# Opening of an FFT-mixing and maxout kernel: half the filter doubling by DMA, the second half of the weights loaded later, zT in parts

## The chip, the cores and the metric

One core of a Trainium2 chip runs the whole program. Its engines work side by side, each on its own queue of instructions in order, and wait for each other by semaphores: TensorE (PE, matmuls; PEld is its weight load), VectorE (DVE), ScalarE (ACT), GpSimd (POOL) and SyncE (SP, which only issues DMAs here; GpSimd issues DMAs too). The metric is the device time of one execution in microseconds (us), less is better.

## The reference

The input x has 8 batches of 3072 positions by 256 channels. Each batch goes through a real FFT along the positions, is multiplied by a filter (`filt_r + i filt_i`, one value per frequency and channel), and is transformed back. Each of the 24576 resulting tokens then goes through a small expert layer with 1024 hidden units.

```
X = np.fft.rfft(x, axis=1)
Y = X * (filt_r + 1j * filt_i)
y = np.fft.irfft(Y, n=3072, axis=1)          # tokens of 256 channels
h1, h2 = y @ w1, y @ w2                      # 256 x 1024 each
out = np.maximum(h1, h2) @ w_out             # 1024 x 256
```

## The kernel before, in words

**The transform as matmuls.** The FFT of 3072 = 96 x 32 is made of small matmuls with tables of sines: C1 (96 points) and U (32 points with the twiddles) forward, VP, VQ (32) and G1 (96) backward. All tables are made at the start of the kernel from index ramps (`table_c`, `tables_u`, `sines_u`, `table_v`, `table_g`). The filter multiplies the half-transformed data elementwise: `product` forms `pq = px * F`, with px in PSUM (the output of `s2`) and F, the filter, in SBUF. F is loaded into partitions 0 to 31 of each half (`load_f`, 16 DMAs that GpSimd issues) and has to stand a second time in partitions 32 to 63 (`double_f`, L124 to L131): for the frequencies w = 0 to 8 by four copies on VectorE (L128), for w = 8 to 12 by four DMAs on SyncE (L130). `fix_f` (L145) sets one row by hand.

**The expert layer.** max(h1, h2) = relu(h1 - h2) + h2. So the kernel keeps Wd = w1 - w2 (`prep_wd`, four parts on GpSimd, L298), computes ph = y Wd (L482), takes its relu into `gt` (L484 on VectorE, L486 on ScalarE) and adds gt w_out (L536) and y M, where M = w2 w_out is made once (`prep_t`, `prep_m`, from `w2b`, the cast of w2, L291).

**Batch 0 by a short way.** Batches 1 to 7 pass through DRAM between the stages of the transform while the expert layer of the batch ahead runs. Batch 0 has nothing to hide behind: it is done at once in SBUF, and this is the opening. Its steps are `s1t` (first matmuls, as the x loads land), `t1` (transposes into `bt`), six times `s2` (matmuls with U into px), `product` (two for each v from 0 to 5, s = 0 and s = 1), `s3t` (matmuls with VP and VQ; evicted to zT, L595 and L597), then `t2` (transposes of zT into `zr`, four rows at a time), and `s4` (matmuls with G1 into py; evicted as `y_`, L464 on ScalarE and L466 on VectorE). The first `ph` needs both halves of the first y tile.

**Who does which product.** VectorE reads px from PSUM. For the products that GpSimd does, ScalarE first copies px to SBUF (`stage_x`, tiles xs). Of the six s = 1 products GpSimd does those in POOLED = (0, 2, 3, 4) and a quarter of that of v = 5 (`shared_product`), VectorE the rest and all of s = 0.

**Order.** The order of instructions on each engine is that of the program text; nothing is rescheduled. A tile comes from a pool with a fixed number of buffers, and its first writer waits until the last reader of what lay there before is done. The pool `init` holds what only the opening needs; `setup.close()` frees it, and the pools of the main loop (`apool`, `ypool` and others) are laid over it. The weights w1 and w2 are loaded by SyncE in two halves of 512 columns (`load_w`, L287 and L288) into WS, a buffer of the long-lived pool `zrpool`.

**Behind the opening** comes the main loop over 65 tiles of 384 tokens, eight steps j each; `plan` and `mid` give the step at which each piece of other work (the remaining `t2`, `f1` of batch 1, and so on) stands. `f1(1, c)` is the first transform step of batch 1: a matmul into pa (L330), an eviction to `at` (L333, L335) and, for odd c, a DMA to DRAM (L338, SyncE). Four of them stand in front of the loop, with two `spin` matmuls that compute nothing.

On GpSimd, behind the last product, stand: the x load (1, 2), the Wo load, Wd part 0, two x loads, Wd parts 1 to 3, the two casts to `w2b`, and the table CT. On SyncE: the filter's last rows, the four doublings, the four weight loads, then the `ad` writes.

Of the kernel before, what the change touches and what calls it, by code (L numbers as in the profile page):

```python
# [8 lines left out]
FP32 = mybir.dt.float32  # L9
BF16 = mybir.dt.bfloat16  # L10
AF = mybir.ActivationFunctionType
OP = mybir.AluOpType
# [15 lines left out]
def kernel(  # L28
# [92 lines left out]
                    o_ = F[64 * g + r0:64 * g + r0 + 16, ri, w0:w1].rearrange("p w s d -> p (w s) d")  # L121
                    G.dma_start(out=o_[:, n0:n], in_=src)

    def double_f(h, g, ri, engine):  # L124
        w0, w1 = WP[h]
        o_, i_ = F[64 * g + 32:64 * g + 64, ri, w0:w1], F[64 * g:64 * g + 32, ri, w0:w1]
        if engine is V:
            V.tensor_copy(o_, i_)  # L128
        else:
            nc.sync.dma_start(out=o_, in_=i_)  # L130
# [11 lines left out]
        G.tensor_copy(F[0:32, ri, 0, 0], FZ[0:32, ri])  # L142

    def fix_f():
        V.tensor_copy(F[32:33, 0, 0, 0], FZ[32:33, 0])  # L145


    V.memset(W1, 1.0)
# [5 lines left out]
    jb = init.tile([128, 16], FP32)  # L154
    cid = init.tile([128, 128], FP32)

    hv = init.tile([128, 2, 1], FP32)
    load_x(0, 0, 1)
    G.iota(pid, pattern=[[1, 1]], base=0, channel_multiplier=1, allow_small_or_imprecise_dtypes=True)
# [32 lines left out]

    def table_ct():
        G.memset(CT, 0.0)
# [55 lines left out]

    def table_g():
        pg = ps.tile([96, NP], FP32, tag="ps", name="pg")
        TE.matmul(pg, C1, I128[0:NP, 0:NP], start=True, stop=True)
        S.activation(G1, pg, AF.Copy)

    def table_v(h, q):
# [22 lines left out]
            S.activation(tab[:, 6 * h + i0:6 * h + 6, s], pv[s][:, i0:6], AF.Copy)  # L279


    WS = zrpool.tile([128, 4, HID], FP32, tag="zr", name="WS")
    w1f, w2f = WS[:, 0:2], WS[:, 2:4]

    def load_w(h):
        js = slice(512 * h, 512 * h + 512)
        nc.sync.dma_start(out=w1f[:, :, js], in_=moe_w1.rearrange("(c p) j -> p c j", p=128)[:, :, js])  # L287
        nc.sync.dma_start(out=w2f[:, :, js], in_=moe_w2.rearrange("(c p) j -> p c j", p=128)[:, :, js])  # L288

    def cast_w2(h):  # L290
        G.tensor_copy(w2b[:, :, 512 * h:512 * h + 512], w2f[:, :, 512 * h:512 * h + 512])  # L291

    def load_wo():
        G.dma_start(out=Wo, in_=moe_w_out.rearrange("(c p) j -> p c j", p=128))

    def prep_wd(q, engine):
        js = slice(256 * q, 256 * q + 256)
        engine.tensor_tensor(Wd[:, :, js], w1f[:, :, js], w2f[:, :, js], OP.subtract)  # L298

    def prep_t(jp):  # L300
        pt = ps.tile([128, 4, D], BF16, tag="ps", name="pt")
# [18 lines left out]
    zd = {}  # L320
    at_ = {}

    def f1(b, c, engine):
        if c == 0:
# [3 lines left out]
        at = at_[b]  # L328
        pa = ps.tile([96, 2, D], FP32, tag="ps", name="pa")
        TE.matmul(pa, C1, xb[b, c // 2][:, 2 * (c % 2):2 * (c % 2) + 2], start=True, stop=True)  # L330
# [57 lines left out]
    def product(E, v, s, px, pool=None):  # L388
        pq = (pool or pqpool).tile([128, 2, 2, D], BF16, tag="pq", name="pq")
        E.tensor_tensor(pq, px.rearrange("p (o i) d -> p o i d", o=1).to_broadcast([128, 2, 2, D]),  # L390
                        F[:, :, 2 * v:2 * v + 2, s], OP.mult)
        return pq

    def shared_product(v, s, px, xs_, pool):
        pq = pool.tile([128, 2, 2, D], BF16, tag="pq", name="pq")
        V.tensor_tensor(pq[:, 0], px, F[:, 0, 2 * v:2 * v + 2, s], OP.mult)
        V.tensor_tensor(pq[:, 1, 0], px[:, 0], F[:, 1, 2 * v, s], OP.mult)
        G.tensor_tensor(pq[:, 1, 1], xs_[:, 1], F[:, 1, 2 * v + 1, s], OP.mult)
        return pq

    def s3(b, v, pq):
# [174 lines left out]

    def s3t(v, pq):
        pool, tag = (ps, "ps") if v % 2 else (pso, "po")
        pz = [pool.tile([128, 2, 2, 2, 2, NM], FP32, tag=tag, name="pt%d" % g) for g in range(2)]
        for _ in range(2 if v == 1 else 1):  # L580
            TE.matmul(pz[0].rearrange("p i s r c m -> p (i s r c m)"), W1[:, 0:128], W1, start=True, stop=True)  # L581
        for i in range(2):
            for s in range(2):
                for dc in range(2):
                    for q, tab in enumerate((VP, VQ)):
                        for g in range(2):
                            TE.matmul(pz[g][:, i, s, :, dc], pq[s][64 * g:64 * g + 64, q, i, 128 * dc:128 * dc + 128],  # L587
                                      tab[64 * g:64 * g + 64, 2 * v + i, s].rearrange("p (r m) -> p r m", r=2),
                                      start=(q == 0), stop=(q == 1))
        zv = zT.rearrange("p c m (w g) q -> p w g (c m) q", g=2)  # L590
        for g in range(2):
            o_ = zv[:, 2 * v:2 * v + 2, g]
            i_ = pz[g].rearrange("p i s r c m -> p i (c m) (s r)")
            if v >= 4 and g == 1:
                V.tensor_copy(o_, i_)  # L595
            else:
                S.activation(o_, i_, AF.Copy)  # L597

    def t2(c, engines):
        if c == 0:  # L600
# [2 lines left out]
        for k, engine in enumerate(engines):  # L603
            pr = ps.tile([96, n, D], BF16, tag="ps", name="pr")
            m0 = 4 * c + n * k
            for m in range(n):
                for dc in range(2):
                    TE.transpose(pr[:, m, 128 * dc:128 * dc + 128], zT[:, dc, m0 + m].rearrange("p u q -> p (u q)"),  # L608
                                 I128)
            if engine is V:  # L610
                V.tensor_copy(zr[0][:, m0:m0 + n], pr)
# [13 lines left out]
    for g in range(2):  # L625
        for ri in range(2):
            double_f(1, g, ri, nc.sync)
    for h in range(2):
        load_w(h)
    spin(12)  # L630
    for c in range(8):
        s1t(c)
# [4 lines left out]
        if c < 7:  # L637
            spin(2)
    bt[0] = bpool.tile([128, NU, D], BF16, tag="bt", name="bt")
    zT = bpool.tile([128, 2, NM, NU, 4], BF16, tag="bt", name="zT")  # L640
    for n in range(6):
        t1(n, S if n % 2 else V)
    put_v(0, 0, table_v(0, 0))
    for g in range(2):
        for ri in range(2):
            double_f(0, g, ri, V)
    fix_f()
    xs = {}

    def stage_x(v):  # L650
        t_ = init.tile([128, 2, D], FP32, name="xs%d" % v)
        S.activation(t_, pxs[v][1], AF.Copy)
        xs[v] = t_

    POOLED = (0, 2, 3, 4)

    def products(v):
        pool = pq0 if v > 2 else pqpool
        pq = [product(V, v, 0, pxs[v][0], pool)]
        if v == 5:  # L660
            pq.append(shared_product(v, 1, pxs[v][1], xs[v], pool))
        else:
            pq.append(product(G, v, 1, xs[v], pool) if v in POOLED else product(V, v, 1, pxs[v][1], pool))
        return pq

    pqs = {}
    pxs = {v: s2(0, v) for v in (1, 0)}
    stage_x(0)
    put_v(0, 1, table_v(0, 1))
    pxs[2] = s2(0, 2)  # L670
    stage_x(2)
    sines_u(1)
    put_v(1, 0, table_v(1, 0))
    pxs[3] = s2(0, 3)
    stage_x(3)
    put_v(1, 1, table_v(1, 1))
    for v in (1, 0, 2):
        pqs[v] = products(v)
        if v == 0:
            load_x(1, 0, 2)  # L680
# [39 lines left out]

    todo = {}
# [30 lines left out]
    plan(0, 9, prep_m)  # L752
    for c, n in ((2, 7), (4, 22), (5, 32), (6, 40), (7, 48)):
        plan(0, n, t2, c, (V,))
    plan_f1(0, 1, (5, 6, 7, 7, 9, 9, 10, 10, 11, 11, 12, 12), 13)
    plan_f2(0, (25, 28, 31, 35, 38, 42, 46), ((0,), (), (1,), (2,), (3,), (4,), (5, 6)),
            (8, 8, 10, 12, 17, 20, 24, 28), (10, 13, 16, 20, 24, 27, 30, 33))
# [71 lines left out]
```

## Time and profile before

| | |
|---|---|
| time, median of 3 runs | 497.97 us (497.71 to 498.13) |
| time of the profiled execution | 498.64 us |
| its span | 496.8 us |
| TensorE busy | 483.8 us (97%) |
| VectorE, ScalarE, GpSimd busy | 335.4, 320.4, 258.7 us |
| granted TensorE clock, mean | 0.989 |
| chain that ended last, share of TensorE | 92% |

The span is what the profile covers; the execution's own time is 1.8 us longer, and the median of the runs is 0.67 us below the profiled execution. The page's slices are a fortieth of the span each, 12.4 us, with busy shares in tenths; PEclk is the clock that was granted to TensorE. A row of a timeline has the start, the busy time, the engine, the line and the operation with its output and inputs, the shape, how many instructions are merged in the row, and in brackets the idle time ahead of the first of them with what ended it.

### The profile page before, as it was taken

Reading aid. Unit: us, or ns where it says so; the run is one execution under the profiler, and the core shown is the slowest. Engines: PE = TensorE matmul, PEld = TensorE weight load, DVE = VectorE, ACT = ScalarE, POOL = GpSimd, SP = SyncE. Lnnn points to the kernel's source line nnn. Section 1 sums busy time; section 2 is a strip of 40 time slices with the busy share of each in tenths; the row PEclk is TensorE's granted clock in tenths of the full one; section 3 lists DMA queues with packets and bytes.
Section 4 is the critical chain, followed back from the end, with each engine's and each line's share of the span. In section 5 each row is a group of like instructions: output and inputs, shape, how many; then the busy total and the mean of one; then the engine's idle time right before and its main releaser. Section 6 shows DMA issues by size and latency. Waiting matters only on the chain.

```text
span 496.8 us, 14137 instructions
## 1 busy us (share of the span) xinstructions
PE 483.8 (97%) x5759; PEld 353.5 (71%) x5759; DVE 335.4 (68%) x535; ACT 320.4 (64%) x667; POOL 258.7 (52%) x342
## 2 busy tenths in 40 slices
PE   7699999999999999999999999999999999999997
PEld 3457777777777777777777777776777777777775
DVE  7886788468855688467855688457873688556542
ACT  5777478667775677576866668665766656464442
POOL 8694868318466594528646295536842212222220
PEclk9879999999999999999999999999999999999999
DMA  8989988996789867896789977897776834531112
GB/s 128 161 242 224 259 269 260 284 234 190 204 266 221 216 210 223 249 225 174 231 257 227 183 244 211 257 215 168 227 231 175 181 104 129 157 120 66 64 64 86
DMA packets 76626, 97.30 MB, mean 196 GB/s; under 512 B 7985, under 2 KB 54354, under 8 KB 75186
## 3 DMA queue, kind: packets, MB, share of 16 engines
q1 hardware_dynamic: 63218, 66.71, 52.1%
q0 software_dynamic: 13200, 29.60, 21.4%
q8 instruction: 45, 0.74, 0.7%
q14 instruction: 19, 0.16, 0.1%
q10 hardware_dynamic: 144, 0.09, 0.1%
HBM read 53.87 MB, written 47.19 MB: 203 GB/s over the span
## 4 chain that ended last, share of the span: by engine, by line
PE 92%; DMA 3%; ACT 2%; POOL 1%; issue 1%; DVE 0%; SPq 0%; POOLq 0%
PE po L536 34%; PE ph L482 33%; PE po L534 8%; PE pz L408 5%; PE pc L443 3%; PE px L384 2%; PE pa L355 2%; DMA xb<-in_x_dram 2%; DMA zr<-zd 1%; PE pt L587 1%; DMA zd<-zt 1%; PE pr L608 1%; POOL xb L89 1%; PE pt L581 1%; PE pa L330 1%
## 5 line engine op out<-in xcount | busy, mean ns | idle before, releaser
L486 ACT ACTIVATE gt<-ph 128x384 bf16<-128x384 f32 x357 | 175.7, 496 | 138.8 <-PE ph L482 136.2
L536 PE MATMUL po<-Wo,gt 128*128 128x256 bf16 x1528 | 262.7, 273 | 1.2 <-issue 1.2
L536 PEld LDWEIGHTS <-gt 128*128 128x128 bf16 x1528 | 144.7, 98 | 68.1 <-issue 13.5
L495 POOL DMA_DIRECT2D out_dram<-ot x186 | 103.1, 558 | 154.7 <-DVE ot L547 138.7
L390 DVE TENSOR_TENSOR pq<-px,F 128x1024 bf16<-128x1024 f32 x91 | 106.9, 1218 | 25.7 <-PE px L384 25.4
L484 DVE TENSOR_SCALAR gt<-ph 128x384 bf16<-128x384 f32 x155 | 83.6, 551 | 53.5 <-PE ph L482 47.1
L482 PEld LDWEIGHTS <-Wd 128*128 128x128 bf16 x1024 | 99.6, 98 | 13.7 <-issue 0.3
L104 POOL TENSOR_TENSOR xb<-XF 128x512 bf16<-128x512 f32 x48 | 61.3, 1277 | 66.9 <-DMA XF<-in_x_dram 31.7
L547 DVE TENSOR_SCALAR ot<-po 128x512 f32<-128x512 f32 x83 | 57.0, 686 | 35.0 <-PE po L536 33.1
L105 POOL TENSOR_TENSOR xb<-XF 128x512 bf16<-128x512 f32 x48 | 61.1, 1274 | 0.0
L359 ACT ACTIVATE at<-pa 128x512 bf16<-128x512 f32 x96 | 51.8, 611 | 3.4 <-PE pa L355 3.3
L412 ACT ACTIVATE zt<-pz 128x512 bf16<-128x512 f32 x84 | 45.6, 594 | 5.7 <-PE pz L408 1.9
L448 ACT ACTIVATE ce<-pc 128x384 f32<-128x384 f32 x56 | 23.7, 490 | 6.7 <-PE pc L443 6.0
L408 PE MATMUL pz<-pq,VP 64*64 64x256 bf16 x336 | 22.2, 281 | 0.0
L384 PE MATMUL px<-bt,U 64*64 64x256 bf16 x384 | 20.4, 283 | 1.2 <-ACT VQ L279 0.7
L408 PE MATMUL pz<-pq,VQ 64*64 64x256 bf16 x336 | 21.1, 269 | 0.0
L408 PEld LDWEIGHTS <-VP 64*64 64x64 bf16 x336 | 10.0, 105 | 13.3 <-issue 12.7
L355 PE MATMUL pa<-xb,CT 64*64 64x512 bf16 x192 | 18.0, 377 | 0.0
L443 PEld LDWEIGHTS <-zr 48*128 48x128 bf16 x896 | 13.1, 93 | 4.8 <-issue 4.4
L443 PE MATMUL pc<-G,zr 48*128 48x48 bf16 x896 | 15.4, 180 | 0.3 <-DMA zr<-zd 0.3
L384 PEld LDWEIGHTS <-U 64*64 64x64 bf16 x384 | 10.6, 109 | 3.9 <-issue 3.6
L618 PE MATMUL pd<-W 128*128 128x512 bf16 x28 | 9.2, 437 | 1.5 <-DVE zero L150 1.5
(383 smaller groups left out, 632.1 us busy)
## 6 DMA issues: line engine op xcount, KB each, us to landing
out_dram<-ot POOLq DMA_DIRECT2D x186, 128.0 KB, 3.8
XF<-in_x_dram SPq DMA_DIRECT2D x96, 192.0 KB
ad<-at SPq DMA_DIRECT2D x56, 192.0 KB
zd<-zt SPq DMA_DIRECT2D x42, 256.0 KB
zr<-zd SPq DMA_DIRECT2D x56, 192.0 KB
bt<-ad SPq DMA_DIRECT2D x13, 768.0 KB
WS<-in_moe_w_dram SPq DMA_DIRECT2D x4, 512.0 KB
xb<-in_x_dram POOLq DMA_DIRECT2D x8, 192.0 KB, 5.6
```

The costliest lines, as they stand in the source:

```text
L104: G.tensor_tensor(t_[:, 0], f[:, 0], f[:, 1], OP.add)
L105: G.tensor_tensor(t_[:, 1], f[:, 0], f[:, 1], OP.subtract)
L359: S.activation(at[:, m0:m0 + 2], pa[g], AF.Copy)
L390: E.tensor_tensor(pq, px.rearrange("p (o i) d -> p o i d", o=1).to_broadcast([128, 2, 2, D]), F[:, :, 2 * v:2 * v + 2, s], OP.mult)
L408: TE.matmul(pz[g][64 * s:64 * s + 64, i], tab[64 * g:64 * g + 64, 2 * v + i, s], pq[s][64 * g:64 * g + 64, q, i], start=(q == 0), stop=(q ...
L412: S.activation(zt[:, :, g], pz[g], AF.Copy)
L482: TE.matmul(ph, Wd[:, dc, 128 * j:128 * j + 128], y_[:, dc], start=(dc == 0), stop=(dc == 1))
L484: V.tensor_scalar(gt[tt][:, j], ph, 0.0, None, OP.max)
L486: S.activation(gt[tt][:, j], ph, AF.Relu)
L495: E.dma_start(out=dst, in_=ot[tt // 2][:, 3 * (tt % 2) + c])
L536: TE.matmul(p_, g_[:, n - 2, blk], Wo[:, n - 2], start=(e == 0), stop=(e == 9))
L547: V.tensor_scalar(ot[tt // 2][:, e - 1:e + 1], po[q // 2 % 2], SCALE, None, OP.mult)
```

## The change

- `double_f` takes the frequencies w0 to w1 now. VectorE doubles w = 0 to 8 for the first half of the partitions (g = 0) and w = 0 to 4 for the second; SyncE's DMAs double w = 4 to 8 for g = 1, ahead of w = 8 to 12 for both. `fix_f` goes to GpSimd.
- A second sine table CP holds C1's columns in another order; G1 is made from CP, and zT has its columns in the order g, w, q instead of w, g, q, and its rows m in eight groups of four. `s3t` evicts the last v in two parts, the first group of rows and then the other seven.
- The sines of U's second half and the matmuls of `table_v(1, 0)` stand earlier.
- POOLED is (0, 2, 3, 5): GpSimd does the whole s = 1 product of v = 5, VectorE that of v = 4.
- The second half of w1 and w2 is loaded behind GpSimd's third product (v = 3), into a tile `wh` of the pool `init`, whose buffer holds the staged px of v = 3 until then.
- On GpSimd the first x load of batch 1 stands behind product v = 2 instead of product v = 0. Behind its last product the order is Wd part 0, x load, Wd part 1, Wo load, Wd part 2, x load, Wd part 3, x load, the two casts.
- `f1` is split into its matmul `f1_in` and its eviction `f1_out`; the evictions of c = 0 and 1 stand behind `s4(0)`, those of c = 2 and 3 behind the first step of the loop. Four `fill` matmuls with a tile of their own replace the two `spin`.

```diff
-    def double_f(h, g, ri, engine):
-        w0, w1 = WP[h]
+    def double_f(w0, w1, g, ri, engine):
...
-        V.tensor_copy(F[32:33, 0, 0, 0], FZ[32:33, 0])
+        G.tensor_copy(F[32:33, 0, 0, 0], FZ[32:33, 0])
...
+        S.activation(CP.rearrange("p (g w c) -> p g w c", g=2, c=4),
+                     uc.rearrange("p (w g s) r -> p g w (s r)", g=2, s=2), AF.Sin, bias=zero[0:NP], scale=TWO_PI)
...
     def load_w(h):
+        wh[h] = init.tile([128, 2, 2, 512], FP32, tag="wh", name="wh") if h else WS
         js = slice(512 * h, 512 * h + 512)
...
+        for k, w in enumerate((moe_w1, moe_w2)):
+            nc.sync.dma_start(out=wh[h][:, k], in_=w.rearrange("(c p) j -> p c j", p=128)[:, :, js])
...
+        for o0, o1 in ((0, 1), (1, 8)) if v == 5 else ((0, 8),):
+            for g in range(2):
+                o_ = zT[:, o0:o1, :, :, g, 2 * v:2 * v + 2].rearrange("p o c m w q -> p o (c m) (w q)")
+                i_ = pz[g][:, o0:o1].rearrange("p o i s r c m -> p o (c m) (i s r)")
...
-    for g in range(2):
-        for ri in range(2):
-            double_f(1, g, ri, nc.sync)
-    for h in range(2):
-        load_w(h)
+    for w0, w1 in ((4, 8), (8, 12)):
+        for g in range(w0 == 4, 2):
+            for ri in range(2):
+                double_f(w0, w1, g, ri, nc.sync)
+    load_w(0)
...
+    sines_u(1)
     for n in range(6):
         t1(n, S if n % 2 else V)
     put_v(0, 0, table_v(0, 0))
+    pv1 = table_v(1, 0)
     for g in range(2):
         for ri in range(2):
-            double_f(0, g, ri, V)
+            double_f(0, 4 if g else 8, g, ri, V)
...
-        t_ = init.tile([128, 2, D], FP32, name="xs%d" % v)
+        if v == 3:
+            t_ = init.tile([128, 2, 2, 512], FP32, tag="wh", name="wh")[:, 0, 0].rearrange("p (i d) -> p i d", i=2)
+        else:
+            t_ = init.tile([128, 2, D], FP32, name="xs%d" % v)
...
-    POOLED = (0, 2, 3, 4)
+    POOLED = (0, 2, 3, 5)
...
     pxs[4] = s2(0, 4)
-    stage_x(4)
+    load_x(1, 0, 2)
     pqs[3] = products(3)
-    s3t(0, pqs[0])
+    load_w(1)
     pxs[5] = s2(0, 5)
     stage_x(5)
+    s3t(0, pqs[0])
...
+    prep_wd(0, G)
     load_x(1, 2, 2)
+    prep_wd(1, G)
     load_wo()
-    prep_wd(0, G)
-    for c in (4, 6):
-        load_x(1, c, 2)
-    for q in range(1, 4):
-        prep_wd(q, G)
+    prep_wd(2, G)
+    load_x(1, 4, 2)
+    prep_wd(3, G)
+    load_x(1, 6, 2)
...
-    f1(1, 0, S)
-    spin(1)
+    f1_in(1, 0)
+    fill(1)
     t2(0, (V, S))
-    f1(1, 1, V)
-    spin(1)
+    f1_in(1, 1)
+    f1_in(1, 2)
+    fill(1)
     s4(0)
-    f1(1, 2, S)
-    f1(1, 3, V)
+    f1_in(1, 3)
+    f1_out(1, 0, S)
+    f1_out(1, 1, V)
+    fill(2)
```

More of the change, by code (lines that the diff above doesn't have):

```diff
@@ L155 @@
     cid = init.tile([128, 128], FP32)
+    CP = init.tile([NP, 96], BF16)
     hv = init.tile([128, 2, 1], FP32)
@@ L252, in table_g @@
         pg = ps.tile([96, NP], FP32, tag="ps", name="pg")
-        TE.matmul(pg, C1, I128[0:NP, 0:NP], start=True, stop=True)
+        TE.matmul(pg, CP, I128[0:NP, 0:NP], start=True, stop=True)
         S.activation(G1, pg, AF.Copy)
@@ L279, in put_v @@
             S.activation(tab[:, 6 * h + i0:6 * h + 6, s], pv[s][:, i0:6], AF.Copy)
-    WS = zrpool.tile([128, 4, HID], FP32, tag="zr", name="WS")
-    w1f, w2f = WS[:, 0:2], WS[:, 2:4]
+    WS = zrpool.tile([128, 4, HID], FP32, tag="zr", name="WS")[:, 0:2].rearrange("p k (c j) -> p k c j", c=2)
+    wh = {}
     def load_w(h):
+        wh[h] = init.tile([128, 2, 2, 512], FP32, tag="wh", name="wh") if h else WS
         js = slice(512 * h, 512 * h + 512)
-        nc.sync.dma_start(out=w1f[:, :, js], in_=moe_w1.rearrange("(c p) j -> p c j", p=128)[:, :, js])
-        nc.sync.dma_start(out=w2f[:, :, js], in_=moe_w2.rearrange("(c p) j -> p c j", p=128)[:, :, js])
+        for k, w in enumerate((moe_w1, moe_w2)):
+            nc.sync.dma_start(out=wh[h][:, k], in_=w.rearrange("(c p) j -> p c j", p=128)[:, :, js])
     def cast_w2(h):
-        G.tensor_copy(w2b[:, :, 512 * h:512 * h + 512], w2f[:, :, 512 * h:512 * h + 512])
+        G.tensor_copy(w2b[:, :, 512 * h:512 * h + 512], wh[h][:, 1])
     def load_wo():
@@ L296, in prep_wd @@
     def prep_wd(q, engine):
-        js = slice(256 * q, 256 * q + 256)
-        engine.tensor_tensor(Wd[:, :, js], w1f[:, :, js], w2f[:, :, js], OP.subtract)
+        w = wh[q // 2][:, :, :, 256 * (q % 2):256 * (q % 2) + 256]
+        engine.tensor_tensor(Wd[:, :, 256 * q:256 * q + 256], w[:, 0], w[:, 1], OP.subtract)
     def prep_t(jp):
@@ L321, with f1_in, f1_out @@
     at_ = {}
+    pas = {}
     def f1(b, c, engine):
+        f1_in(b, c)
+        f1_out(b, c, engine)
+    def f1_in(b, c):
+        pas[c] = ps.tile([96, 2, D], FP32, tag="ps", name="pa")
+        TE.matmul(pas[c], C1, xb[b, c // 2][:, 2 * (c % 2):2 * (c % 2) + 2], start=True, stop=True)
+    def f1_out(b, c, engine):
         if c == 0:
@@ L327, in f1 @@
             at_[b] = apool.tile([128, 8, D], BF16, tag="at", name="at")
-        at = at_[b]
-        pa = ps.tile([96, 2, D], FP32, tag="ps", name="pa")
-        TE.matmul(pa, C1, xb[b, c // 2][:, 2 * (c % 2):2 * (c % 2) + 2], start=True, stop=True)
+        at, pa = at_[b], pas.pop(c)
         o_ = at[0:96, 2 * (c % 4):2 * (c % 4) + 2]
@@ L391, in product @@
                         F[:, :, 2 * v:2 * v + 2, s], OP.mult)
[L392 to L398, printed above, removed]
         return pq
@@ L578, in s3t @@
         pool, tag = (ps, "ps") if v % 2 else (pso, "po")
-        pz = [pool.tile([128, 2, 2, 2, 2, NM], FP32, tag=tag, name="pt%d" % g) for g in range(2)]
+        pz = [pool.tile([128, 8, 2, 2, 2, 2, 4], FP32, tag=tag, name="pt%d" % g) for g in range(2)]
         for _ in range(2 if v == 1 else 1):
-            TE.matmul(pz[0].rearrange("p i s r c m -> p (i s r c m)"), W1[:, 0:128], W1, start=True, stop=True)
+            TE.matmul(pz[0].rearrange("p o i s r c m -> p (o i s r c m)"), W1[:, 0:128], W1, start=True, stop=True)
         for i in range(2):
@@ L586, in s3t @@
                         for g in range(2):
-                            TE.matmul(pz[g][:, i, s, :, dc], pq[s][64 * g:64 * g + 64, q, i, 128 * dc:128 * dc + 128],
-                                      tab[64 * g:64 * g + 64, 2 * v + i, s].rearrange("p (r m) -> p r m", r=2),
+                            TE.matmul(pz[g][:, :, i, s, :, dc].rearrange("p o r m -> p r o m"),
+                                      pq[s][64 * g:64 * g + 64, q, i, 128 * dc:128 * dc + 128],
+                                      tab[64 * g:64 * g + 64, 2 * v + i, s].rearrange("p (r o m) -> p r o m", r=2, m=4),
                                       start=(q == 0), stop=(q == 1))
-        zv = zT.rearrange("p c m (w g) q -> p w g (c m) q", g=2)
-        for g in range(2):
[L592 to L597, printed above, removed]
+        for o0, o1 in ((0, 1), (1, 8)) if v == 5 else ((0, 8),):
+            for g in range(2):
+                o_ = zT[:, o0:o1, :, :, g, 2 * v:2 * v + 2].rearrange("p o c m w q -> p o (c m) (w q)")
+                i_ = pz[g][:, o0:o1].rearrange("p o i s r c m -> p o (c m) (i s r)")
+                if v >= 4 and g == 1:
+                    V.tensor_copy(o_, i_)
+                else:
+                    S.activation(o_, i_, AF.Copy)
     def t2(c, engines):
@@ L624 @@
     tables_u()
-    for g in range(2):
-        for ri in range(2):
-            double_f(1, g, ri, nc.sync)
-    for h in range(2):
-        load_w(h)
+    for w0, w1 in ((4, 8), (8, 12)):
[3 more added lines that the diff above has]
+    load_w(0)
     spin(12)
@@ L639 @@
     bt[0] = bpool.tile([128, NU, D], BF16, tag="bt", name="bt")
-    zT = bpool.tile([128, 2, NM, NU, 4], BF16, tag="bt", name="zT")
+    zT = bpool.tile([128, 8, 2, 4, 2, NW, 4], BF16, tag="bt", name="zT")
+    sines_u(1)
     for n in range(6):
@@ L659, in products @@
         pq = [product(V, v, 0, pxs[v][0], pool)]
[L660 to L663, printed above, removed]
+        pq.append(product(G, v, 1, xs[v], pool) if v in POOLED else product(V, v, 1, pxs[v][1], pool))
         return pq
@@ L710, with fill @@
     gpool = ctx.enter_context(tc.tile_pool(name="gpool", bufs=2))
-    f1(1, 0, S)
-    spin(1)
+    pd = pso.tile([128, 512], FP32, tag="po", name="pd")
+    def fill(n):
+        for _ in range(n):
+            TE.matmul(pd, W1[:, 0:128], W1, start=True, stop=True)
+    f1_in(1, 0)
+    fill(1)
     t2(0, (V, S))
-    f1(1, 1, V)
-    spin(1)
+    f1_in(1, 1)
+    f1_in(1, 2)
+    fill(1)
     s4(0)
-    f1(1, 2, S)
-    f1(1, 3, V)
+    f1_in(1, 3)
+    f1_out(1, 0, S)
+    f1_out(1, 1, V)
+    fill(2)
     todo = {}
@@ L754 @@
         plan(0, n, t2, c, (V,))
+    plan(0, 0, f1_out, 1, 2, S)
+    plan(0, 0, f1_out, 1, 3, V)
     plan_f1(0, 1, (5, 6, 7, 7, 9, 9, 10, 10, 11, 11, 12, 12), 13)
```

11 lines of the change are left out of this document (5 added, 6 removed).

## The prediction

> **What bounds the kernel now.** I read the slices of the page first, then the timelines of VectorE, GpSimd and TensorE over the first 45 us, then busy time and granted clock in 1 us stretches.
>
> ```profile
> PE   7699999999999999999999999999999999999997
> PEclk9879999999999999999999999999999999999999
> ```
>
> The reader is to see that TensorE is full from the fourth slice (37 us) on. So the time is the moment at which the expert stage (the `ph` and `po` matmuls) begins, plus TensorE's own work after it: a microsecond at the opening's end is a microsecond of the total, and a wait after that point is paid in full.
>
> ```profile
> 18.49 4.76 DVE L128 COPY F<-F 32x4096 bf16<-32x4096 bf16 x4
> 23.28 0.28 DVE L145 CAST F<-XF 1x256 bf16<-1x256 f32 x1
> 23.76 8.13 DVE L390 TENSOR_TENSOR pq<-px,F 128x1024 bf16<-128x1024 f32 x7 [0.19 <-DVE F L145]
> ...
> 37.36 0.56 DVE L466 TENSOR_SCALAR y__998<-py 128x384 bf16<-128x384 f32 x1
> ```
>
> VectorE is full from 18.49 to 32.80: the filter doubling holds the products back. The first y tile is evicted from 37.36, and TensorE's first `ph` runs at 37.73.
>
> ```profile
> 23.43 2.12 POOL L390 TENSOR_TENSOR pq<-xs,F 128x1024 bf16<-128x1024 f32 x1 [1.20 <-DVE F L128]
> 25.50 0.56 POOL L89 DMA_DIRECT2D xb<-in_x_dram  x1
> 26.07 6.30 POOL L390 TENSOR_TENSOR pq<-xs,F 128x1024 bf16<-128x1024 f32 x3
> 32.34 0.66 POOL L398 TENSOR_TENSOR pq<-xs,F 128x256 bf16<-128x256 f32 x1
> ...
> 36.72 3.74 POOL L298 TENSOR_TENSOR Wd<-WS 128x512 bf16<-128x512 f32 x3
> 40.40 2.01 POOL L291 CAST w2b<-WS 128x1024 bf16<-128x1024 f32 x2
> ```
>
> GpSimd is full too, with work that nobody waits for at once: its last weight cast ends at 42.36, 5 us after the first y. Here that is harmless: y waits for VectorE's products and for its own matmuls, and not for the casts.
>
> **The change, part by part.**
>
> *Doubling.* Two of VectorE's four copies shrink to half and two stay: 4.76 x 3/4 = 3.57, so 1.19 saved. `fix_f` (0.28) goes to GpSimd, where I put 0.5, between its 0.28 on VectorE and the 0.56 of a GpSimd cast of 32x256. VectorE's products start at 18.49 + 3.57 = 22.1 instead of 23.76. SyncE issues two more doublings, ahead of its four (20.79 to 25.03 now, 1.06 each). They are wanted by the v=2 products at about 25; issued near 21, they are late only if landing takes over 4 us (the 64 KB filter loads take 4.2): 0 to 1.2 us of GpSimd's time. I take 0, since these copies need no DRAM; the upper end stays in the range.
>
> *Products.* VectorE gets eight whole ones (8 x 1.16 = 9.3, now 8.13 + 0.68 + 0.41 = 9.2). GpSimd gets four whole ones and no quarter: 8.4 instead of 8.42 + 0.66.
>
> *Second sines.* ScalarE's 0.93 us go into its idle 1.34 us ahead of the `bt` copies, so TensorE's wait of 1.54 us for U at 23.95 goes. What is late next are the products, so nothing of it reaches the end by itself. The extra sine of `CP` (0.38, as C1's) sits ahead of a wait of 1.77 us.
>
> *zT in parts.* The last eviction before the transposes shrinks from 0.69 to an estimated 0.25 (64 of 512 elements a row; between the 0.13 of VectorE's tiniest rows and 0.69): 0.4 saved. The four fills and the `f1` evictions put behind s4(0) stand in idle time of TensorE, if there is a wait there.
>
> *What the opening would then give.* Now 4.4 us pass from the last product (32.99) to the y eviction (37.36); 4.0 with the smaller eviction. GpSimd's last product would end at 31.7 (below), so y at about 35.7; with transposes and py faster, 34.5 at best. That is a gain of 1.7 to 2.9 us, if the first x load lands in time: it moves behind GpSimd's product v=2 (issued 27.0 instead of 25.50), `f1_in(1, 0)`, which reads it, heads TensorE's order in front of the transposes, and the table of DMA issues has 8.4 us as the median landing of these 384 KB. 27.0 + 8.4 = 35.4 would put y at about 38. Either way it is earlier than what follows.
>
> *The weights, and the wait that they add.* The second half of w1 and w2 no longer lies in `WS` (a long-lived pool) but in `wh`, a tile of `init`. That pool is closed ahead of the expert stage, and `ypool` is laid over it: by the program's addresses y's first tile stands at byte 199008 to 200544 of each partition, inside `wh` (196608 to 204800). So in the changed order both evictions of the first y, on ScalarE and VectorE, carry a new wait: for GpSimd's **last cast out of `wh`**, the tenth instruction behind its last product. Now the same evictions wait for no cast. Behind the y evictions stand, on VectorE and ScalarE, the `at` and `gt` evictions; on TensorE the first `ph`, and behind it everything; on SyncE the `ad` writes.
>
> When does that cast end? GpSimd's filter DMA issues end at 22.22 (19.82 + 2.40) as now, since nothing ahead of them moves. Then: 0.5 fix_f, 4 x 2.10 products, 0.56 for the x load between them: 22.2 + 9.5 = 31.7. The inputs are there: the fourth F copy at 22.1, the staged copies of ScalarE 0.2 us or more ahead of each product (v=5's, behind s3t(1) and s2(5), at about 29.5, wanted at 29.65, is the tightest). Behind the last product stand the same ten instructions as now (four `Wd` parts, three x loads, Wo, two casts), only reordered; now they take from 32.99 to 42.36 = 9.4 us with no idle time. 31.7 + 9.4 = **41.1**. `Wd` ahead of the x loads brings only `Wd` forward, which y's wait makes worthless: the sum of the queue is what counts. A wait for the second weights can only add to it: they are issued behind product v=3 (29.65), 1 MB; 24 to 34 us ran at 254 GB/s, so 4.1 us if alone, and they are wanted at 35.7. I take 0 and keep 1.5 us for the range (x and Wo loads share the queues).
>
> So y is evicted from 41.2 instead of 37.36: **+3.85 us**. TensorE stands idle from about 36 (its last matmul ahead of `ph`) to 41.8.
>
> *The clock.* That idle time has a second price, and the trace shows its like:
>
> ```profile
> 20.00:21.00 1.00, 0.82 (x49) 1.00 0.61 68
> 21.00:22.00 1.00, 0.32 (x8) 0.64 0.73 101
> ...
> 25.00:26.00 1.00, 0.79 (x49) 0.50 0.37 82
> 26.00:27.00 1.00, 1.00 (x11) 0.50 0.47 107
> ...
> 30.00:31.00 1.00, 0.89 (x11) 0.50 1.03 285
> 31.00:32.00 1.00, 1.00 (x34) 0.74 1.07 346
> 32.00:33.00 1.00, 1.00 (x34) 1.00 0.99 287
> ```
>
> The columns are the stretch, its length, TensorE's busy time (instructions), the granted clock, and DMA. A thin stretch around 19 to 24 us halves the clock from 21.4, and it comes back only at 31.5: 5.5 us after work had become gapless (26.0), 7.5 us after it came back at all (23.95). After the new wait TensorE has gapless work at full speed now (2.00 busy of 2.00 in each stretch from 38 on, a `ph` pair in 0.33), so half clock for 5.5 us costs 5.5/2 = 2.75, for 7.5 us 3.75; nothing, if the clock should hold. I take **+2.7**, the gapless case being the nearer one.
>
> [...]
>
> **Sum.** +3.85 + 2.7 = +6.6 us. On the profiled execution, 498.64 (span 496.80), that is 505.2; on the median of the runs shown, 497.97, which is 0.67 lower, **504.6**. I predict on the median.
>
> **Rivals.**
> - *The wait without the clock.* The clock holds, or comes back within 2 us: +3.85 to +4.9, 501.8 to 502.9. For it: the clock stayed at 1.00 through the waits of 0.3 to 0.8 us between 5 and 15 us. Against: here about 5 us are empty, where 1 to 3 thin ones were enough at 21.
> - *Second weights or doublings late.* GpSimd stalls in front of the third `Wd` part or of product v=2, by 1 to 3 us, and y with it: 505.6 to 507.6. For it: DMA is at 0.87 or more in this stretch, and a Wo load took 10.6 us to land. Against: the weights' own rate above.
> - *Faster: the opening's gain stays.* The wait for the casts decides only if GpSimd's last cast ends after about 35.7, when y would be ready anyway. Were it over by then, 1.7 to 2.9 us would remain, if the x load lands in time too: 495.1 to 496.3, say 495.6. It needs GpSimd's 9.4 us behind the products to shrink to 4. Against: these rows have one length wherever they stand (the 128x512 ones 1.26 to 1.29 over the whole span), and TensorE's transposes of `w2b` start at 41.64 now, just behind the first cast, so the records are no illusion.
>
> **Chances.** Wait and clock 0.75 (504.6; its own range 503 to 506); wait without clock 0.11; late loads 0.08; faster 0.06. The range leaves out the faster case, half of the lightest waits and the worst of the late loads: 501.5 to 507.0. A measurement of this kernel can tell about 0.2% (1 us) from no change. Faster 0.06, same 0.01, slower 0.93.
>
> **What would show it.** In the changed profile: VectorE's first product near 22.1; GpSimd's last product ending near 31.7 and its second `w2b` cast near 41.1, with no idle time between; both y evictions starting within 0.1 us of that end and put down to GpSimd; TensorE empty from 36 to 41.8; a granted clock of 0.5 somewhere from 37 to 48; the rest of the span as now, later. I am wrong if y starts ahead of the second cast, or if TensorE has slack behind 42 us that takes the shift in.

## The result, and the profile after

The changed kernel takes 504.17 us (median of 6 runs, 503.79 to 506.81), beside 498.02 us for the kernel before (6 runs, 497.36 to 498.92). By the medians that is 6.15 us slower, where +6.6 was forecast. The ratio, worked out from all the runs, is 1.0136, with a 95% interval of 1.0111 to 1.0160 (+6.8 us, 5.5 to 8.0), so it is slower clear of the noise. The profiled execution of the changed kernel is one of its longer ones: 505.77 us, span 504.0, mean clock 0.982.

The slices of the page, TensorE and its granted clock, show the main difference in the fourth slice (37.8 to 50.4 us), which is thinner and colder than before. The third is a little thinner and colder too, the first two differ by a tenth, and all behind the fourth is as full as it was.

```profile
PE   8685999999999999999999999999999999999997
PEclk9967999999999999999999999999999999999999
```

The timeline of VectorE (start, busy time, line, operation, tiles; in brackets the idle time ahead and what ended it) has the shorter doubling and the earlier products, as forecast. Then it shows two holes.

```profile
18.76 3.70 DVE L127 COPY F<-F 32x4096 bf16<-32x4096 bf16 x4
22.56 5.75 DVE L401 TENSOR_TENSOR pq<-px,F 128x1024 bf16<-128x1024 f32 x5
28.50 3.49 DVE L401 TENSOR_TENSOR pq<-px,F 128x1024 bf16<-128x1024 f32 x3 [0.20 <-PE px L395]
35.43 0.69 DVE L600 CAST zT<-pt 128x512 bf16<-128x512 f32 x1 [3.44 <-PE pt L591]
...
43.89 0.56 DVE L470 TENSOR_SCALAR y__997<-py 128x384 bf16<-128x384 f32 x1 [6.35 <-POOL w2b L294]
```

The products are over at 31.99 (32.81 before), and still the next thing VectorE can do is at 35.43, because `pt` comes late from TensorE. The first y then waits 6.35 us for GpSimd's cast into `w2b`. GpSimd's own timeline says when that cast ends:

```profile
29.71 2.13 POOL L401 TENSOR_TENSOR pq<-xs,F 128x1024 bf16<-128x1024 f32 x1
34.37 1.28 POOL L301 TENSOR_TENSOR Wd<-WS 128x512 bf16<-128x512 f32 x1 [2.53 <-DMA WS<-in_moe_w_dram]
...
42.81 1.05 POOL L294 CAST w2b<-wh 128x1024 bf16<-128x1024 f32 x1
```

The last product ends at 31.84 (29.71 + 2.13) and the last cast at 43.86 (42.81 + 1.05). In front of the first `Wd` part GpSimd stood idle for 2.53 us, for the first half of the weights: the forecast had no idle time there. The list of waits from 14 to 58 us has the whole path in three lines (waiting engine and line, what released it, us in total, times, longest):

```profile
DVE y__997 L470 <- POOL w2b L294: 6.3, 1, 6.3
PE ph L486 <- ACT y__997 L468: 5.4, 1, 5.4
POOL Wd L301 <- DMA WS<-in_moe_w_dram: 2.5, 1, 2.5
```

And the table by microseconds (TensorE busy, granted clock, DMA) has the second price, a clock that falls in the empty time and is paid behind it:

```profile
41.00:42.00 1.00, 0.00 (x0) 0.81 1.45 200
42.00:43.00 1.00, 0.00 (x0) 0.50 1.50 191
...
47.00:48.00 1.00, 1.00 (x5) 0.50 0.85 283
48.00:49.00 1.00, 1.00 (x13) 0.78 0.26 90
49.00:50.00 1.00, 1.00 (x7) 1.00 0.00 0
```

**The account, on the two profiled executions.** First y 37.36 to 43.89, +6.53. First `ph` 37.73 to 44.44, +6.71. First eviction of a finished output tile (`ot`) 53.91 to 62.48, +8.57; so behind the first `ph`, with the clock at 0.50 up to 48.4 us, the shift grew by 1.86. The shift of the `ot` evictions stays between +8.57 and +8.48 until about 325 us and then drops to +7.27, where it stays to the end (491.01 to 498.28). The drop has two steps. The first, 0.46, is in before's execution the end of a wait for the load of a `zr` tile, which the changed one doesn't have; whether that is chance or slack one pair of traces doesn't show. The second, 0.76, are holes that the profile puts down to nothing ("issue"), 1.23 us long before and 0.47 after (two rows of before, then one of after):

```profile
325.98 0.77 PE L443 MATMUL pc<-G,zr 48*128 48x48 bf16 x47 [0.28 <-DMA zr<-zd]
...
336.35 0.28 PE L536 MATMUL po<-Wo,gt 128*128 128x256 bf16 x1 [1.23 <-issue]
```

```profile
343.24 0.34 PE L486 MATMUL ph<-y__6518,Wd 128*128 128x384 bf16 x1 [0.47 <-issue]
```

So a single pair of traces can differ by about a microsecond in the main loop, and what the change does is best read up to the first tiles.

### The profile page after: what moved, and what is told of

Its sections match the earlier page's. It is cut to its first block, busy times and chain, and to the rows that moved or that the text cites. A ratio compares the mean times of both kernels' runs of the same rounds, so it can differ in the third digit from the quotient of the medians.

```text
span 504.0 us, 14150 instructions
## 1 busy us (share of the span) xinstructions
PE 486.3 (96%) x5757; PEld 355.9 (71%) x5761; DVE 334.7 (66%) x534; ACT 320.3 (64%) x668; POOL 258.5 (51%) x342
## 4 chain that ended last, share of the span: by engine, by line
PE 90%; DMA 4%; POOL 4%; issue 1%; SPq 0%; ACT 0%; DVE 0%; POOLq 0%
PE po L540 34%; PE ph L486 34%; PE po L538 8%; PE pz L412 5%; PE pc L447 3%; PE pa L366 2%; PE px L395 2%; DMA xb<-in_x_dram 2%; DMA WS<-in_moe_w_dram 1%; POOL xb L89 1%; POOL Wd L301 1%; DMA F<-in_filt_i_dram 1%; POOL F L122 1%; PE pr L613 1%; PE pa L334 1%
## 5 line engine op out<-in xcount | busy, mean ns | idle before, releaser
L401 DVE TENSOR_TENSOR pq<-px,F 128x1024 bf16<-128x1024 f32 x92 | 108.1, 1219 | 25.8 <-PE px L395 25.5
L104 POOL TENSOR_TENSOR xb<-XF 128x512 bf16<-128x512 f32 x48 | 61.3, 1277 | 70.6 <-DMA XF<-in_x_dram 41.6
```

What stands on the lines that cost most here:

```text
L104: G.tensor_tensor(t_[:, 0], f[:, 0], f[:, 1], OP.add)
```

## The experiments

Theory A: the place of the second weights half (`wh` in `init`, under `ypool`) makes the first y wait for GpSimd's last cast, and this, with the clock behind it, is the whole loss. Rival B: the loss comes from lateness, that is, from weights, doublings and x loads that arrive later, wherever they lie. Rival C: the rest of the opening's new order is slower by itself. In the results, "us" is the median, and the ratio, worked out from all runs, is to the kernel before, measured beside it; in brackets stands its 95% interval.

### The place: taken away, alone, and in doses

**e1, the changed kernel with the second half in another place.** WS has an unused half of its buffer; the second weights and the staged px of v = 3 go there. Nothing else moves.

```diff
-        wh[h] = init.tile([128, 2, 2, 512], FP32, tag="wh", name="wh") if h else WS
+        wh[h] = WS[:, h]
```

> The changed kernel with one thing undone: the second half of the weights (and the staged px of v=3, that shares its place) lies in the unused half of WS, in the long-lived pool, instead of in wh. All loads, orders and waits for product v=3 stay. Theory A (the place: y waits for the last cast out of wh): in the changed kernel's profile py ends at 38.3, so y is evicted from about 38.3 instead of 43.9, the clock stays up, and the time falls from 504.2 to about 499 to 500 (0.9 us behind the kernel before, which has y at 37.36, plus up to 1 for Wd parts that end at 37.4, 39.6 and 41.4). Rival B (lateness: the wait only covers weights and products that are late by themselves, through the added DMA traffic and the half clock): y starts early, but ph stalls on Wd, and the time stays above 502.

Measured: 499.13 us, ratio 1.0024 (1.0011 to 1.0038). Five of the six microseconds are gone, though the loads stand where they stood in the order. On VectorE and TensorE:

```profile
37.94 0.56 DVE L470 TENSOR_SCALAR y__995<-py 128x384 bf16<-128x384 f32 x1 [0.97 <-PE py L464]
```

```profile
38.34 0.87 PE L486 MATMUL ph<-y__995,Wd 128*128 128x384 bf16 x4
```

y is released by its own matmul now, while GpSimd's last casts still run from 40.67 to 42.69. GpSimd still waits for weights, 0.67 us for the first half and 1.07 for the second, and y doesn't wait for it. Theory A holds, B falls as the main cause. What is left, +0.24%, and a y that is not sooner than 37.36, are a second question (below).

**e2, the kernel before with the place alone.** Only the second half of w1 and w2 moves, to a tile of `init`; the load stays where it was.

```diff
+        wh[h] = init.tile([128, 2, 2, 512], FP32, name="wh") if h else WS
```

> The kernel before with one part of the change alone: the second half of the weights lies in a tile wh of the pool init; its load, and every order, stay. Theory A: the first writer over init now waits for the last cast, which ends at 42.4. In this order that is the at eviction ahead of the zr eviction on ScalarE (35.21 now), so zr follows at 43, py and y near 44, 6.6 us later than 37.36, plus 2 to 3 us of half clock, less about 1 us that is won back later: 504.5 to 507.5. Rival B: nothing moves a load or a product, so the time is the kernel before's, 498.0 within 1 us.

Measured: 506.2 us, 1.0157 (1.0131 to 1.0183). The place alone costs about as much as the whole change (the two intervals overlap). On ScalarE, then GpSimd:

```profile
44.13 0.59 ACT L337 ACTIVATE at<-pa 96x512 bf16<-96x512 f32 x1 [7.68 <-POOL w2b L293]
```

```profile
31.98 2.13 POOL L392 TENSOR_TENSOR pq<-xs,F 128x1024 bf16<-128x1024 f32 x1 [1.33 <-ACT xs L654]
...
43.06 1.03 POOL L293 CAST w2b<-wh 128x1024 bf16<-128x1024 f32 x1
```

The trace of ScalarE tells why it isn't less. In the old order the `f1` evictions stand in front of the first `zr` and y evictions, and `at` too meets the wait for the cast. So the wait sits one step earlier, and the eviction of `zr`, py and y come behind it one after the other: the cast ends at 44.09, y starts on ScalarE at 45.64. In the changed kernel, whose `f1` evictions stand behind `s4(0)`, these 1.55 us are 0.03. One part of this execution's wait isn't the place's: GpSimd and VectorE both start their products of v = 4 at 31.98, GpSimd behind a wait of 1.33 us, although the staged px was done at 29.51. Of their inputs only the doubled filter is left, so the cast's end, 44.09 and not 42.36 as before, has late doublings in it.

**e4, the changed kernel with the casts sooner.** The x loads of GpSimd's queue go behind the casts.

```diff
     prep_wd(2, G)
-    load_x(1, 4, 2)
     prep_wd(3, G)
+    cast_w2(1)
+    cast_w2(0)
+    load_x(1, 4, 2)
     load_x(1, 6, 2)
-    for h in range(2):
-        cast_w2(h)
```

> The changed kernel with GpSimd's order behind the last Wd load changed: Wd part 2, part 3, the cast out of wh, the cast out of WS, and then the two x loads (0.55 and 0.54) that stood between; nothing else. The cast out of wh then ends 0.55 + 0.54 + 1.0 = 2.1 us sooner (41.7 instead of 43.8). Theory A: y starts 2.1 us sooner, and the time falls by 2.1, to 502.1 (by up to 1 us more if the shorter idle time shortens the half clock). Rival B: the order of casts has no reader that waits for it, so the time stays at 504.2.

Measured: 501.99 us, 1.0084 (1.0057 to 1.0112). The cast out of `wh` ends at 41.30, and y starts at 41.34 (GpSimd, then VectorE):

```profile
40.27 1.03 POOL L294 CAST w2b<-wh 128x1024 bf16<-128x1024 f32 x1
```

```profile
41.34 0.56 DVE L470 TENSOR_SCALAR y__997<-py 128x384 bf16<-128x384 f32 x1 [3.15 <-POOL w2b L294]
```

y is 3.98 us later than before, and the time is 3.7 us longer by the medians, 4.2 by the ratio. Here the clock stayed at 1.00 behind the wait (TensorE was empty for 2.15 us): without the clock's price the time grew by about what y is late.

### The clock's share: what could not be settled by times

**e3 and e5, the changed kernel with more fills.** 28 (e3) or 18 (e5) matmuls of 128x512 that compute nothing run while y waits, instead of 2. The diff is that of e3.

```diff
-    fill(2)
+    fill(28)
```

> The changed kernel with 28 instead of 2 fill matmuls (128x512, 0.216 us each) in front of the first ph: 26 x 0.216 = 5.6 us of work without use, which fills TensorE's empty 38.8 to 44.4. It leaves the wait as it is and takes the clock's part away. Theory A with its clock term: y and ph start as in the changed kernel (43.9 and 44.4), the clock stays at 1.00, and the 1.9 us go that the half clock cost between 44.4 and 48.3: 502.3. If the clock has no part in the loss: 504.2, the same.

Measured: 504.14 us, 1.0121 (1.0098 to 1.0143).

```profile
38.89 6.21 PE L722 MATMUL pd<-W 128*128 128x512 bf16 x28
44.94 0.81 PE L486 MATMUL ph<-y__997,Wd 128*128 128x384 bf16 x4
```

The clock stayed at 1.00 there, and the shift did not grow behind the first `ph` (+7.21, then +7.13), where the changed kernel's grew by 1.86. But in this execution the weights landed early, y was done at 42.8, and the fills were what `ph` waited for. The time says nothing on the clock.

> The changed kernel with 18 instead of 2 fill matmuls in front of the first ph: 16 x 0.216 = 3.5 us, which end at about 42.3, ahead of the y evictions (42.2 to 43.9), so that they delay nothing; with 28, the first ph had to wait for the fills. Theory A with its clock term: ph starts as in the changed kernel, at full clock, and up to 1.9 us go: 502.3 to 503. If the half clock behind the wait has no part in the loss: 504.2.

Measured: 507.28 us, 1.0174 (1.0139 to 1.0209), no better than without fills. In its profiled execution the first weights landed late (first `Wd` part at 34.63), y started at 44.17, the fills were over at 42.1, and after 2.58 empty us the clock was at half from 44.8 to 48.2. Of its four runs one took 503.58 and the other three 507.27 to 508.29. That the clock costs 1 to 2 us is read from the traces: from the first `ph` to the first `ot` the shift grows by 1.86 (after), 1.59 (e5) and 0.90 (e2), and by 0.2 or less in e3 and e4, which stay at full clock. The half clock lasted 4.0, 3.4 and 2.0 us behind the first `ph`, so the shift grew by 0.45 to 0.47 of its length each time. No pair of times here isolates it.

### Parts of the opening alone

**e7, e8, e9: the kernel before with zT in parts; with the doubling, `fix_f` and early sines; with both.** Weights, GpSimd's order and the split of products stay as before.

> The kernel before with one part alone: CP, the new order of zT's columns and rows, and the eviction of the last v in two parts. The forecast gives it 0.4 us (0.69 to 0.25 for the piece that the first transposes wait for): 497.8 against 498.2. If the small evictions cost as much as they save (0.22 each, two per engine, and the second one stands ahead of the zr eviction): no difference.

Measured: 497.77 us, 1.0003 (0.9988 to 1.0018). (In its trace the doubling starts 0.95 later than in before's and y 0.69, at 38.05, with the same median: the start of one execution moves by as much as such an edit.)

> The kernel before with one part alone: half of the second doubling by DMA, fix_f on GpSimd, U's second sines and table_v(1, 0) earlier; products, weights, zT and the f1 order stay. VectorE's products then start 1.2 to 1.6 us sooner. If the products set the end of the opening (the forecast's reason for a gain of 1.3 us): 497.0. If the s3t chain of TensorE at half clock does: s3t(1) starts 0.8 us sooner and s3t(5) at best as much, 497.5 to 498.2, and the products only end with more idle time behind them.

Measured: 497.34 us, 0.9995 (0.9984 to 1.0006); y on VectorE at 37.11 instead of 37.36.

> The kernel before with all parts of the change that leave the weights, the GpSimd order and the split of the products alone: half the doubling by DMA, the early sines and table_v(1, 0), CP, zT's other order and its eviction in two parts. One theory: what bounds the opening is the chain of s3t and its evictions on TensorE and ScalarE; then the smaller last eviction is the only thing that can show, first y at about 36.7 to 37.0 (was 37.36), 497.0 to 497.5 us. Rival: the earlier products matter, but only together with the smaller eviction; then first y at 36.2 or earlier, 496.5 us or less. If neither shows, 497.8.

Measured: 497.70 us, 0.9998 (0.9985 to 1.0011). No part gives a gain that can be measured, alone or together. Yet in the trace of e9 y starts at 36.39, 0.97 sooner than before. VectorE, GpSimd, then TensorE:

```profile
30.11 2.36 DVE L392 TENSOR_TENSOR pq<-px,F 128x1024 bf16<-128x1024 f32 x2 [2.14 <-DMA F<-F]
...
36.39 0.56 DVE L468 TENSOR_SCALAR y__1004<-py 128x384 bf16<-128x384 f32 x1
```

```profile
30.13 2.14 POOL L392 TENSOR_TENSOR pq<-xs,F 128x1024 bf16<-128x1024 f32 x1 [0.81 <-DMA F<-F]
```

```profile
38.37 0.82 PE L484 MATMUL ph<-y__1004,Wd 128*128 128x384 bf16 x4 [0.27 <-POOL Wd L300]
39.83 0.50 PE L484 MATMUL ph<-y__1004,Wd 128*128 128x384 bf16 x2 [0.64 <-POOL Wd L300]
```

Two things are late next. The products of v = 4 need the frequencies w = 8 and 9, which SyncE's DMAs double. SyncE issues six doublings here, until 26.05 (before: four, until 25.03). They land at 30.1, and VectorE, sooner by 1.5 us, waits 2.14 for them. And the `ph` matmuls, sooner by 1 us, wait 0.9 for the `Wd` parts. The first `ot` eviction is 0.41 later than before.

**e11, e9 with the clock kept up.** The runs so far left one explanation open: in all these traces a good part of `s3t` runs at half clock. Here 18 more matmuls that compute nothing are put into the thin stretch, and GpSimd's order has `Wd` ahead of the x loads.

```diff
     def s2(b, v, fills=0):
+        for _ in range(fills):
+            TE.matmul(px[0].rearrange("p i d -> p (i d)"), W1[:, 0:128], W1, start=True, stop=True)
...
-    pxs = {v: s2(0, v) for v in (1, 0)}
+    pxs = {v: s2(0, v, 3) for v in (1, 0)}
```

> The kernel before with half the doubling by DMA, the early sines, CP and zT in parts as in the run with these parts together, GpSimd's order Wd ahead of the x loads as in the changed kernel (the weights stay in WS), and 18 more matmuls that compute nothing (14 of 128x512 ahead of s2 for v = 1, 0, 2, 3, 4 and 4 of 128x384 in table_v), about 0.2 us each at full clock. If the half clock of the opening, and not the products, is what holds y, and thin work on TensorE at 18 to 24 us is what brings it: no stretch at 0.5 before 30 us, s3t at full clock, first y at 35 to 36 us, 495.5 to 496.8 us. If the clock falls all the same: y at 37 to 38 us, 497.5 to 499. If the products or the doublings' landing bound it: clock at 1.00, but VectorE not idle between products except for F, y at 36.5 to 37.5, about 497.5.

Measured: 499.19 us, 1.0023 (1.0007 to 1.0039). The clock is 1.00 in every stretch from 17 to 50 us (mean over the span 1.000), and the time is no better. VectorE, GpSimd, then TensorE:

```profile
30.82 2.35 DVE L396 TENSOR_TENSOR pq<-px,F 128x1024 bf16<-128x1024 f32 x2 [3.46 <-PE pt L593]
36.86 0.56 DVE L472 TENSOR_SCALAR y__1022<-py 128x384 bf16<-128x384 f32 x1
```

```profile
30.84 2.13 POOL L396 TENSOR_TENSOR pq<-xs,F 128x1024 bf16<-128x1024 f32 x1 [1.83 <-DMA F<-F]
```

```profile
45.77 0.60 PE L542 MATMUL po<-Wo,gt 128*128 128x256 bf16 x4 [0.89 <-DMA Wo<-in_moe_w_out_dram]
```

VectorE is idle for 3.46 us and starts on v = 4 at 30.82. The profile names TensorE, but GpSimd starts its product of v = 4 at 30.84, put down to the doubling DMA. So it is the doubling again that both wait for. y is 0.50 sooner than before, and then `po` waits 0.89 for Wo, whose load now stands behind two `Wd` parts (issued at 36.57 instead of 33.51). So the half clock is not the bound alone: with it gone, the doublings and Wo are. As GpSimd's order was changed in the same run, its time doesn't say what the clock alone is worth.

**e10, e9 without the fills in `s3t`.** Seven matmuls of 128x512 less, on the chain that was thought to bind.

> The kernel before with the same parts of the change, and without the seven matmuls of 128x512 in s3t that compute nothing (0.32 us each at full clock, 0.54 to 0.59 at half). If TensorE's own chain at half clock bounds the opening, about 7 x 0.55 = 3.9 us less work stand on it, of which part lay in waits: first y 1 to 2 us sooner, 495.5 to 496.5 us. If these matmuls hold the clock up, the half-clock stretch grows and the time is as without this edit or 0.5 to 2 us more.

Measured: 499.46 us, 1.0027 (1.0009 to 1.0046), slower. In its trace the half clock lasts from 22.5 to 39.6, 17 us instead of 6.8 in e9, and y starts at 39.31, though the doublings' landing (31.8) has a part in that. So without these matmuls the kernel is slower and not faster, and the trace has the longer half clock that the rival asks for. How much of the loss is the clock's and how much the doublings' isn't settled.

### What is left in e1

**e6, e1 with `s2(5)` and its staging behind `s3t(0)` as before; e12, e1 with both weights halves loaded at once and the x loads and GpSimd's order as before.**

> The kernel with the weights' place undone (499.1) and one more part undone: s2 and the staging of v=5 stand behind s3t(0) again, as in the kernel before. In its profile TensorE's chain from s3t(1) to s3t(5), at half clock up to 34, sets the y eviction (37.8 to 37.9), and the products are done 3 us ahead of it; s2(5) ahead of s3t(0) costs this chain a wait of 0.33 for a zT eviction and holds s3t(0) back by 0.5. If the s3t chain is the bound: 0.5 us less, 498.6. If the products bound it (the forecast's reason): v=5's product on GpSimd gets later by 1 to 1.5 us, and the time rises to 499.5 or more.

Measured: 499.66 us, 1.0029 (1.0014 to 1.0044), which can't be told from e1 and is not the gain of 0.5: not that order. GpSimd's product of v = 5 then waits 2.01 us for its staged px, and y starts at 38.23 (e1: 37.94).

> As the run with the second weights half in another place, but both halves loaded at once as in the kernel before, the staged px of v = 3 in a tile of its own, and the x loads and GpSimd's order as before. Kept: POOLED (0, 2, 3, 5), the doubling, zT, the f1 split and the fills. If the +0.9 us that were left there come from the late weights and the late first x load: 498.0 to 498.4 us, as the kernel before. If they come from the order of s2(5) and s3t, from the other split of the products or from f1's order: 499.0 to 499.5.

Measured: 499.31 us, 1.0030 (1.0010 to 1.0049). Putting the loads back gains nothing, but it isn't a clean test: in its trace the doublings land late (VectorE waits 2.35 us and starts on v = 4 at 30.83), which e1's trace does not have, so a gain may have been eaten up there. Beside e9 this kernel has the other split of the products, the order of `s2(5)`, and the `f1` split with its fills. Which of these costs the 0.3% isn't settled.

## Why the prediction was right, point by point

- **The wait, its place and its size.** Right, and shown by e1 (gone with the place), e2 (there with the place alone) and e4 (as long as the cast is late). Both y evictions start at 43.89, 0.03 after the last cast.
- **The end of the last cast.** Forecast 41.1, in the profiled execution 43.86. The queue was right nearly term by term: last product 31.84 (forecast 31.7), behind it 9.5 us of work (43.86 - 31.84 - 2.53; forecast 9.4). The failed term is "I take 0" for late weights, and in this execution it failed at the first half, not at the second, which the forecast had in mind (in e1 and e3 GpSimd waited for the second half too, 1.07 and 0.56). SyncE issues the first half behind the last doubling, and that end varies: where it issued at 25.1 to 25.5 (e3, e1) `Wd` could start at 32.2, where it issued at 26.3 to 26.4 (e4, after, e5) at 33.9 to 34.6. Before, it issued at 25.07, behind four doublings, and nobody waited. So the wait for the cast was +6.5 in this execution and +4.9 in that of e3, where y came at 42.25.
- **The clock.** Forecast 2.7, measured 1.86, 1.59 (e5) and 0.90 (e2). The half clock came, from 41.6 to 48.4, but only 4.0 us of that (44.44 to 48.4) had work in it. The 5.5 us taken from before's row all counted as work; here the other 2.8 us at half clock (41.6 to 44.44) passed while TensorE was empty.
- **The sum.** +6.6 forecast, +6.15 measured. In the profiled pair 6.71 + 1.86 - 1.30 = 7.27: a wait larger than forecast, a clock smaller, and the drop in the main loop. The mechanism was right; that the sum came within half a microsecond is in part luck, as the errors of the two terms have opposite signs.
- **The opening without the wait.** Wrong, though it did not decide. I put y at 35.7 (34.5 at best; 38 with a late x load); e1 and e6 have 37.94 and 38.23, and in the changed kernel py was over at about 38.3. The failed step: the 4.4 us from last product to y were read in a stretch at full clock (before's came back at 31.5) and carried over to one where `s3t` ran at half clock to 34.8. The products were over, and `pt` was not. From the last product to y it took 6.3 us in e1, and 2.8 in e11, whose clock stayed up; no run changes the clock alone, so its share is argued and not shown. The late x load was not the reason: the matmul that reads it starts at 36.19 without a wait. So the rival "faster: the opening's gain stays" had no gain to keep. And it is luck that the empty stretch had nearly the forecast length (39.1 to 44.4, forecast 36 to 41.8): its start and its end were both late, by 3.1 and 2.6 us.
- **Doublings at nothing.** The text has them "wanted by the v=2 products at about 25", with up to 1.2 us. In the changed kernel's trace they were in time. In e9, e10, e11 and e12, which load all the weights right behind them, they hold the products of v = 4 (v = 5 for GpSimd in e12) until 30.1 to 31.8, and VectorE waits 2.1 to 3.5 us. In e8 and e2 both engines start late in the same way (30.2 and 32.0). So the bound was looked for at the wrong product. The reason given for 0, that these copies need no DRAM, was an assumption: no run shows that they land sooner for it (the 64 KB filter loads, out of DRAM, took 4.2). Counted from the end of SyncE's issue, the doublings of these six land 4.1 to 5.4 us later; in the kernels that load the second half of the weights later (after, e1, e3 to e6) they are there within 3.1 us, though in e5 VectorE still waited 1.63 for them. That this delay spares the doublings fits these traces, one execution each; no run tests it alone, and before and e7, which load all the weights at once too, show no such wait.
- **"No slack behind 42 us".** Right in the main: the shift shrinks by 0.1 up to 325 us and by 1.2 at the two places told above, of which only the 0.46 at the `zr` load could be slack.

## What to carry to other kernels

A tile that moved into a pool which is closed and overlaid handed its last reader to the first writer of what lies above: y waited 6.35 us for a cast in the changed kernel and for none in e1. So take the end of that reader's queue and set it against the moment at which the new writer would be ready. Moving one of several chains that end within a microsecond or two of each other can buy nothing until the next ones are moved as well (in e9 y is 0.97 us sooner, the ratio 0.9998): here products, doublings, TensorE's clock, `Wd` and Wo took turns. And read a duration between two events only where the clock was what it will be in the new place: from the last product to y it was 4.4 us before, with the clock at 1.00 from 31.5, and 6.3 in e1, at half until 33.9.

## What the runs showed of the hardware that had not been expected

The half-clock stretches, worked out from the granted clock of the stretches at their ends, are 6.8 us long (e2, e7, e9), 10.2 (before, after, e1, e6, e8), 13.7 (e3, e4, e5, e12) and 17.1 (e10) in the opening, and 6.8 (after, e2) and 3.4 (e5) behind the wait. Each is one execution, so which length goes with which edit is not known. Where one execution has two falls they lie 17.06 us apart (after, e2) or 23.90 (e5). Behind an empty stretch of 2.15 us the clock stayed at 1.00 (e4), and behind one of 2.58 it fell to 0.50 (e5).

How little TensorE had to do doesn't settle in these traces whether the clock falls. In before the clock fell at 21.3, behind stretches of 1 us with 0.83, 0.46 and 0.82 us of work (18 to 21 us); in e4 it stayed at 1.00 through 0.72, 0.00 and 0.12 (39 to 42 us). And work didn't bring it back at once: in before it stayed at 0.50 from 26 to 30 us, with TensorE busy 1.00 of each, and in e2 it came back at 48.6, 3.3 us after the first matmul behind the wait (45.26). So whether a wait of 2 to 3 us costs the clock, and for how long, was not shown: no run tests it.
